# Where a kernel converts the second layer's float64 weights: beside the fourth chunk, or beside the second and third

## The chip, the cores and the metric

The kernel runs on one core of one Trainium2 chip. The metric is the device time of one execution in microseconds (us). The engines are TensorE (PE; PEld is its weight load), VectorE (DVE), ScalarE (ACT), GpSimd (POOL) and SyncE (SP), which here issues every DMA. Each engine has its own queue and works through it in order; semaphores tie them together.

## What is computed

Attention in which a query sees only the keys of its own hash bucket, and behind it two feed-forward layers:

```python
def _attn_ref(q, k, v, proj):                    # q, k, v: 2 x 8 x 768 x 64
    q_bits = (np.einsum('bhsd,dk->bhsk', q, proj) > 0)   # 6 bits; k_bits likewise
    mask = q_bucket[:, :, :, None] == k_bucket[:, :, None, :]
    scores = np.where(mask, scale * q @ k.T, -1e9)
    ...
    return np.matmul(softmax(scores), v)

x = attn_out.transpose(0, 2, 1, 3).reshape(1536, 512)
h = np.maximum(x @ w_in, 0.0)                    # layer one: 512 -> 2048 -> 512
x = h * h @ w_out
h = x @ w_in2                                    # layer two
out = (np.maximum(h, 0) + alpha * np.minimum(h, 0)) @ w_out2
```

The four weight matrices come as float64, since the reference divides them by a float64 number; q, k, v and the result are float32.

## The kernel before

**Tiling.** The 1536 tokens go in four chunks of T = 384 (NCH = 4). A layer's weights are cut into 16 steps f (KFF = 16), each with one tile of the first matrix (o = 0) and one of the second (o = 1), 128 partitions by 512 columns; a tile is named by u = (layer, f, o), so a layer has 32.

**A feed-forward chunk** is `feed_forward(l, c, background)`. For each f it splits two weight tiles into a high and a low part (`split`, L496, `split_w`, L457: ScalarE writes the high part, L462, VectorE or POOL the low one, L463), multiplies the hidden block in three products (`hidden`, L510 to L512), forms the activation in a high and a low part (L518 to L528; L528 on POOL), and multiplies the block of the step before into the accumulator (`project`, L538, L539, L542). At its end VectorE and ScalarE copy the accumulator out (L592, L594).

**Where weights come from.** `fetch(i)` (L476) brings the tiles of step i, two steps ahead of their use. In the first chunk of layer one they are converted: `load_bits` (L431) reads 512 KB of float64 as pairs of 32-bit words, `to_f32` (L437) makes float32 of them: ScalarE scales the upper words into `we` (L444), VectorE takes the sign (L446), joins the upper bits of the lower word (L447) and joins the two (L448). The result goes to DRAM (`w_d`, L494), and the later chunks of layer one read it from there (L488). `keep(u)` (L452) does the same conversion for a tile of layer two and leaves it in SBUF until the end.

**What runs beside what.** `Background(steps, marks)` holds a list of steps, and marks that say how many of them have to have run by which time; time counts in chunks, a chunk has 16 x 5 = 80 slots, and each call of `step()` in `feed_forward` moves it by one slot. The first chunk's attention runs alone. Attention for chunks two to four runs beside the layer-one chunks one to three, each ready at 0.8 of the chunk before (LEAD). Beside the fourth chunk and the first 0.3 of layer two's first chunk run the 32 `keep` steps (L649), and `second_x`, which transposes a layer-one result for layer two, at 0.3 to 0.7 of a chunk.

**Buffers.** `weight_pools` makes the pools for weights: `whole` holds four float32 tiles, `conv` the conversion's `we` and `wsg`, `wide` the tiles of 512 KB (three while attention runs, eight later). When attention is over, its pools and these are closed, and made anew with other sizes; `res` then holds the 32 kept tiles.

Of the kernel before, what the change touches and what calls it, by code (L numbers as in the profile page):

```python
# [7 lines left out]
F32 = mybir.dt.float32  # L8
# [21 lines left out]
def kernel(  # L30
# [20 lines left out]
    nc = tc.nc  # L51
    B, H, D, S = qT.shape
    NB = N_BITS
    NT, DM = out.shape
    P = 128
# [4 lines left out]
    NCH = NT // T  # L60
    KDM = DM // P
    KFF = w_in1.shape[0]
# [4 lines left out]
    def pool(name, bufs, stack=ctx, **kw):  # L67
        return stack.enter_context(tc.tile_pool(name=name, bufs=bufs, **kw))

    const = pool("const", 1)  # L70
    dram = pool("scr", 1, space=DRAM)
# [3 lines left out]
    ps_m = pool("ps_m", 2, space=PSUM)  # L75
    m1 = pool("m1", 1)
    m2 = pool("m2", 2)
    weights = ctx.enter_context(ExitStack())
    att = ctx.enter_context(ExitStack())
    state = {"attention": True, "moe": False, "s": 0, "m": 0, "h": 0}  # L80

    def weight_pools(stack, late):

        if not late:
            state["whole"] = pool("whole", 4, stack)
        state["conv"] = pool(f"conv{late}", 1 + late, stack)
        state["parts0"] = pool(f"parts0{late}", 2 + late, stack)
        state["parts1"] = pool(f"parts1{late}", 2, stack)
        state["wide"] = pool(f"wide{late}", 8 if late else 3, stack)

    weight_pools(weights, 0)
    p1 = pool("p1", 1, att)
    p2 = pool("p2", 2, att)
# [333 lines left out]
    w_d = {}  # L427
    kept = {}
    y_d = {}

    def load_bits(u):  # L431
        l, f, o = u
        t = state["wide"].tile([P, DM, 2], U32, tag="wide", name="wbits")
        nc.sync.dma_start(out=t.rearrange("p n b -> p (n b)"), in_=(WO if o else WI)[l][f].bitcast(U32))
        w_bits[u] = t

    def to_f32(u, w):  # L437


        if u not in w_bits:  # L440
            load_bits(u)
        t = w_bits.pop(u)
        e = state["conv"].tile([P, DM], F32, tag="we", name="we")
        nc.scalar.activation(e, t[:, :, 1].bitcast(F32), AF.Copy, scale=2.0 ** -112)  # L444
        s = state["conv"].tile([P, DM], U32, tag="wsg", name="wsg")
        nc.vector.tensor_scalar(s, t[:, :, 1], 0x80000000, None, ALU.bitwise_and)  # L446
        nc.vector.scalar_tensor_tensor(s, t[:, :, 0], 29, s, ALU.logical_shift_right, ALU.bitwise_or)  # L447
        nc.vector.scalar_tensor_tensor(  # L448
            w.bitcast(U32), e.bitcast(U32), 3, s, ALU.logical_shift_left, ALU.bitwise_or
        )  # L450

    def keep(u):  # L452

        kept[u] = state["res"].tile([P, DM], F32, name="w%d_%d_%d" % u)
        to_f32(u, kept[u])

    def split_w(u, engine):  # L457
        w = w_f.pop(u)
# [10 lines left out]
    def units(i):  # L469

        if i >= len(work):
            return []
        l, c, f = work[i]
        return [(l, f, o) for o in range(2)]

    def fetch(i):  # L476

        for u in units(i):
            if u in kept:
                w_f[u] = kept[u]  # L480
            elif u in w_d:
                if state["attention"]:
                    w = state["whole"].tile([P, DM], F32, tag="wf", name="wf")
                else:

                    w = state["wide"].tile([P, DM, 2], U32, tag="wide", name="wf")
                    w = w.rearrange("p n b -> p (n b)")[:, 0:DM].bitcast(F32)
                nc.sync.dma_start(out=w, in_=w_d[u])  # L488
                w_f[u] = w
            else:  # L490
                w_f[u] = state["whole"].tile([P, DM], F32, tag="wf", name="wf")
                to_f32(u, w_f[u])
                w_d[u] = dram.tile([P, DM], F32, tag="w%d_%d_%d" % u, name="w%d_%d_%d" % u)
                nc.sync.dma_start(out=w_d[u], in_=w_f[u])  # L494

    def split(i, o):  # L496
        for u in units(i)[o:o + 1]:
            split_w(u, nc.gpsimd if o or i // KFF == 1 else nc.vector)

    def hidden(l, c, f, x, step):  # L500
        xh, xl = x
        wih, wil = w_split.pop((l, f, 0))
        ps = h_tile()
        hp = ps[:, 0:T]
        for kk in range(KDM):
            if kk == KDM // 2:
                step()
            ks = slice(kk * P, (kk + 1) * P)
            first, last = kk == 0, kk == KDM - 1
            nc.tensor.matmul(hp, wih[:, ks], xh[:, kk, :], start=first, stop=False)  # L510
            nc.tensor.matmul(hp, wih[:, ks], xl[:, kk, :], start=False, stop=False)  # L511
            nc.tensor.matmul(hp, wil[:, ks], xh[:, kk, :], start=False, stop=last)  # L512
        r = m1.tile([P, T], F32, tag="r", name="r")
        g = m1.tile([P, T], F32, tag="g", name="g")
        gh = m2.tile([P, T], F32R, tag="gh", name="gh")
        gl = m2.tile([P, T], F32R, tag="gl", name="gl")
        if l == 0:
            nc.scalar.activation(r, hp, AF.Relu)  # L518
            nc.scalar.activation(gh, r, AF.Square)  # L519
            if SQUARE[c] == "a":  # L520
                nc.scalar.activation(g, r, AF.Square)
            else:
                eng[SQUARE[c]].tensor_tensor(g, r, r, ALU.mult)
        else:
            nc.vector.tensor_scalar(r, hp, 0.0, alpha_sb[:, f:f + 1], ALU.min, ALU.mult)  # L525
            nc.vector.scalar_tensor_tensor(g, hp, 0.0, r, ALU.max, ALU.add)  # L526
            nc.scalar.activation(gh, g, AF.Copy)  # L527
        nc.gpsimd.tensor_tensor(gl, g, f32(gh), ALU.subtract)  # L528
        return gh, gl
# [28 lines left out]
    def feed_forward(l, c, background):  # L558

        slots = KFF * 5  # L560
        state["slot"] = 0

        def step():
            state["slot"] += 1
            background(state["slot"] / slots)

        x = xT.pop((l, c) if l else c)
        pend = None
        acc = None
        for f in range(KFF):  # L570
            i = index[l, c, f]
            split(i + 1, 0)
            split(i, 1)
            g = hidden(l, c, f, x, step)
            fetch(i + 2)
            for u in units(i + 3):
                if u not in w_d and u[0] == 0:
                    load_bits(u)
            step()
            if pend is not None:  # L580
                if acc is None:
                    acc = ps_a.tile([P, 3, 512], F32, tag="acc", name="acc")
                project(l, *pend, acc, step)
            pend = (f, g)
        project(l, *pend, acc, step)
        y = m1.tile([P, NTB, DM], F32, tag="y", name="y")
        if l == 0:
            d = dram.tile([P, NTB, DM], F32, tag=f"y{c}", name=f"y{c}")
            y_d[c] = d
        for t in range(NTB):  # L590
            if t % 2 == 0 or l and c == NCH - 1 and t == NTB - 1:
                nc.vector.tensor_copy(y[:, t, :], acc[:, t, :])  # L592
            else:
                nc.scalar.activation(y[:, t, :], acc[:, t, :], AF.Copy)  # L594
            if l:
                s0 = c * T + t * P
                nc.sync.dma_start(out=out[s0:s0 + P, :], in_=y[:, t, :])
        if l == 0:
            nc.sync.dma_start(out=d, in_=y)
# [33 lines left out]
    steps, marks = [], [(0.0, 0)]  # L633
    for c in range(1, NCH):
        steps += attention(c, 1)
        marks.append((c - 1 + LEAD, len(steps)))
    following = Background(steps, marks)
    for c in range(NCH - 1):
        feed_forward(0, c, lambda x: following(c + x))
    following(NCH)  # L640
    att.close()
    weights.close()
    weight_pools(ctx, 1)
    state["res"] = pool("res", 1)
    state["attention"] = False


    steps = [lambda f=f, o=o: keep((1, f, o)) for f in range(KFF) for o in range(2)]
    conversion = Background(steps, [(0.0, 0), (1.3, len(steps))])  # L649
    for n in range(NCH + 1):  # L650
        steps = second_x(n) if n < NCH else []
        turned = Background(steps, [(0.3, 0), (0.7, len(steps))])
# [75 lines left out]
```

## Time and profile before

| | us |
|---|---|
| median of three runs | 870.07 |
| lowest and highest of the three | 867.12, 870.68 |
| the profiled execution, its own time | 869.21 |
| span of that execution, first to last instruction | 867.4 |
| TensorE, VectorE, ScalarE, POOL busy in it | 810.9, 552.7, 480.6, 378.6 |

Busy time of TensorE is the time covered by its matmuls, whose ends are modelled, since they overlap; it is no measure of how near to its peak it works. A group of instructions is named by its line in the kernel, its engine, and the tiles that it writes and reads (`wsg<-wbits`). Behind the bar stand its busy time, the mean of one in ns, the engine's idle time just before it, and what ended that idle time.

### The profile page before, as it was taken

The numbers are of one execution on the slowest core, as the hardware profiler recorded it, in microseconds if no ns is written. First come the engines' busy times: TensorE is split into PE (matmuls) and PEld (weight loads), VectorE is DVE, ScalarE is ACT, GpSimd is POOL, SyncE is SP. The second block draws the span as 40 slices with busy tenths as digits, with TensorE's granted clock in tenths as the row PEclk, the third lists the DMA queues.
The fourth block names the chain that finished last, engine by engine and source line by source line (L and its number), as shares of the span: only waits on it lengthen the run. The fifth ranks groups of instructions, "written<-read, shape, count | busy, mean of one in ns | idle before, by whom it ended". The sixth has DMA issues, their size and how long they took to land.

```text
span 867.4 us, 12076 instructions
## 1 busy us (share of the span) xinstructions
PE 810.9 (93%) x4192; PEld 653.4 (75%) x4192; DVE 552.7 (64%) x854; ACT 480.6 (55%) x925; POOL 378.6 (44%) x328
## 2 busy tenths in 40 slices
PE   5998998899999999999999998868999999999996
PEld 3655677676768778778777877647998998998995
DVE  6989899997666345366454599978445444444442
ACT  5668668776656556557555656654444444444331
POOL 3011233432646556433332554475555555554553
PEclk7999999999999999999999999989999999999999
DMA  7442766664332233342223777750010010000000
GB/s 232 139 133 96 254 183 210 223 203 133 112 129 71 88 110 80 89 126 85 71 82 88 274 234 259 262 215 37 1 37 37 0 38 37 1 1 37 1 0 37
DMA packets 42989, 96.40 MB, mean 111 GB/s; under 512 B 5200, under 2 KB 13744, under 8 KB 42928
## 3 DMA queue, kind: packets, MB, share of 16 engines
q1 hardware_dynamic: 42928, 95.63, 34.2%
q8 instruction: 33, 0.54, 0.3%
q14 instruction: 28, 0.23, 0.1%
HBM read 80.88 MB, written 14.73 MB: 110 GB/s over the span
## 4 chain that ended last, share of the span: by engine, by line
PE 59%; DVE 9%; issue 4%; ACT 3%; DMA 3%; POOL 2%; SPq 0%; POOLq 0%; DVEq 0%; ACTq 0%
PE acc L542 8%; PE acc L538 7%; PE acc L539 7%; PE m L329 5%; PE h L510 4%; PE h L512 4%; PE h L511 4%; PE m L313 4%; PE m L512 3%; PE m L510 3%; PE m L511 3%; PE s L292 2%; PE s L293 2%; DVE wsg L447 2%; DVE wl L463 2%
## 5 line engine op out<-in xcount | busy, mean ns | idle before, releaser
L528 POOL TENSOR_TENSOR gl<-g,gh 128x384 fp32r<-128x384 f32 x128 | 142.6, 1114 | 266.3 <-ACT gh L527 122.2
L538 PE MATMUL acc<-wh,gh 128*128 128x512 f32 x384 | 162.0, 422 | 12.6 <-ACT gh L519 10.2
L463 POOL TENSOR_TENSOR wl<-wf,wh 128x512 fp32r<-128x512 f32 x80 | 107.7, 1347 | 119.3 <-ACT wh L462 109.0
L539 PE MATMUL acc<-wl,gh 128*128 128x512 f32 x384 | 152.2, 396 | 0.0
L542 PE MATMUL acc<-wh,gl 128*128 128x512 f32 x384 | 117.2, 404 | 9.0 <-POOL gl L528 8.9
L462 ACT ACTIVATE wh<-w 128x512 fp32r<-128x512 f32 x128 | 80.4, 629 | 74.8 <-PE m L511 40.3
L462 ACT ACTIVATE wh<-wf 128x512 fp32r<-128x512 f32 x128 | 79.5, 627 | 56.0 <-PE h L511 28.9
L510 PE MATMUL h<-xh,wh 128*128 128x384 f32 x296 | 107.2, 362 | 1.1 <-ACT xh L357 0.8
L511 PE MATMUL h<-xl,wh 128*128 128x384 f32 x296 | 101.0, 341 | 0.6 <-POOL xl L358 0.6
L512 PE MATMUL h<-xh,wl 128*128 128x384 f32 x296 | 101.2, 342 | 0.0
L296 DVE TENSOR_REDUCE low<-s 128x1 f32<-128x768 f32 x84 | 80.1, 954 | 29.4 <-PE s L293 28.7
L538 PEld LDWEIGHTS acc<-wh,gh 128*128 128x128 f32 x384 | 72.6, 189 | 31.1 <-ACT gh L519 13.0
L542 PEld LDWEIGHTS acc<-wh,gl 128*128 128x128 f32 x384 | 71.9, 190 | 30.8 <-POOL gl L528 15.2
L299 ACT ACTIVATE sm<-s,low 128x768 f32<-128x768 f32 x84 | 75.3, 896 | 27.4 <-DVE low L296 27.1
L313 PE MATMUL m<-ident,sm 128*128 128x128 f32 x528 | 83.0, 274 | 5.8 <-DVE bits L215 4.0
L463 POOL TENSOR_TENSOR wl<-w,wh 128x512 fp32r<-128x512 f32 x64 | 83.9, 1310 | 8.9 <-ACT wh L462 8.6
L313 PEld LDWEIGHTS m<-ident,sm 128*128 128x128 f32 x528 | 65.5, 140 | 21.8 <-DVE bits L215 4.9
L539 PEld LDWEIGHTS acc<-wl,gh 128*128 128x128 f32 x384 | 72.9, 190 | 9.7 <-issue 1.2
L527 ACT ACTIVATE gh<-g 128x384 fp32r<-128x384 f32 x64 | 33.5, 524 | 83.6 <-DVE g L526 83.6
L525 DVE TENSOR_SCALAR r<-m,alpha_sb 128x384 f32<-128x384 f32 x43 | 26.5, 617 | 82.3 <-PE m L512 82.1
L319 DVE COPY pt<-m 128x384 f32<-128x384 f32 x112 | 61.4, 552 | 23.3 <-PE m L313 23.0
L512 PE MATMUL m<-xh,wl 128*128 128x384 f32 x216 | 72.9, 338 | 0.5 <-DVE wl L463 0.5
(105 smaller groups left out, 1568.6 us busy)
## 6 DMA issues: line engine op xcount, KB each, us to landing
wf<-w SPq DMA_DIRECT2D x96, 256.0 KB
wbits<-in_w_in_dram SPq DMA_DIRECT2D x32, 512.0 KB
wbits<-in_w_out_dram SPq DMA_DIRECT2D x32, 512.0 KB
w<-wf SPq DMA_DIRECT2D x32, 256.0 KB
qr<-in_qT_dram SPq DMA_DIRECT2D x32, 192.0 KB
kr<-in_kT_dram SPq DMA_DIRECT2D x8, 384.0 KB
qn<-in_qT_dram SPq DMA_DIRECT2D x16, 192.0 KB
vr<-in_v_dram SPq DMA_DIRECT2D x8, 384.0 KB
```

Source lines behind the costliest of these rows:

```text
L296: nc.vector.tensor_reduce(low, ps[:, 0:2, 0:HALF], AX.XY, ALU.max, negate=True)
L299: nc.scalar.activation(sm.rearrange("p (a n) -> p a n", a=2), ps[:, 0:2, 0:HALF], AF.Exp, bias=low, accum_out=self.sums[:, i:i + 1],)
L313: nc.tensor.transpose(ps[:, i * P:(i + 1) * P], pp[:, b * P:(b + 1) * P], ident)
L462: nc.scalar.activation(hi, w, AF.Copy)
L463: engine.tensor_tensor(lo, w, f32(hi), ALU.subtract)
L510: nc.tensor.matmul(hp, wih[:, ks], xh[:, kk, :], start=first, stop=False)
L511: nc.tensor.matmul(hp, wih[:, ks], xl[:, kk, :], start=False, stop=False)
L512: nc.tensor.matmul(hp, wil[:, ks], xh[:, kk, :], start=False, stop=last)
L528: nc.gpsimd.tensor_tensor(gl, g, f32(gh), ALU.subtract)
L538: nc.tensor.matmul(acc[:, t, :], gh[:, blocks[t]], woh, start=first, stop=False)
L539: nc.tensor.matmul(acc[:, t, :], gh[:, blocks[t]], wol, start=False, stop=False)
L542: nc.tensor.matmul(acc[:, t, :], gl[:, blocks[t]], woh, start=False, stop=last)
```

## The change

The conversion of the 32 tiles of layer two moves out of the fourth chunk. A second list of background steps, beside attention, loads and converts them between the times 1.0 and 2.9, that is beside the second and third layer-one chunk (`ahead`), and stores the float32 tile in DRAM. The conversion's last step now writes over its own input `we`. In the fourth chunk `keep` only reads the stored tile, from 0.25 of the chunk to 0.3 of the next. The pool `whole` now lives until the end, and the later `conv` pool has one buffer in place of two.

```diff
+    state_whole = pool("whole", 4)
...
-        if not late:
-            state["whole"] = pool("whole", 4, stack)
-        state["conv"] = pool(f"conv{late}", 1 + late, stack)
+        state["conv"] = pool(f"conv{late}", 1, stack)
...
-    def to_f32(u, w):
+    def to_f32(u, w=None):
...
+        w = e if w is None else w
         nc.vector.scalar_tensor_tensor(
             w.bitcast(U32), e.bitcast(U32), 3, s, ALU.logical_shift_left, ALU.bitwise_or
         )
+        return w
+
+    def ahead(u):
+
+        w = to_f32(u)
+        w_d[u] = dram.tile([P, DM], F32, tag="w%d_%d_%d" % u, name="w%d_%d_%d" % u)
+        nc.sync.dma_start(out=w_d[u], in_=w)
 
     def keep(u):
 
         kept[u] = state["res"].tile([P, DM], F32, name="w%d_%d_%d" % u)
-        to_f32(u, kept[u])
+        nc.sync.dma_start(out=kept[u], in_=w_d[u])
...
+    steps = []
+    for f in range(KFF):
+        for o in range(2):
+            steps += [lambda u=(1, f, o): load_bits(u), lambda u=(1, f, o): ahead(u)]
+
+    conversion = Background(steps, [(1.0, 0), (NCH - 1.1, len(steps))])
+
+    def beside(x):
+        following(x)
+        conversion(x)
+
     for c in range(NCH - 1):
-        feed_forward(0, c, lambda x: following(c + x))
+        feed_forward(0, c, lambda x: beside(c + x))
+    conversion(NCH)
     following(NCH)
...
     steps = [lambda f=f, o=o: keep((1, f, o)) for f in range(KFF) for o in range(2)]
-    conversion = Background(steps, [(0.0, 0), (1.3, len(steps))])
+    conversion = Background(steps, [(0.25, 0), (1.3, len(steps))])
```

## Rows read from the trace of the kernel before

**Rows 1.** The page: span, and each engine's busy time.

```profile
span 867.4 us, 12076 instructions
PE 810.9 (93%) x4192; PEld 653.4 (75%) x4192; DVE 552.7 (64%) x854; ACT 480.6 (55%) x925; POOL 378.6 (44%) x328
```

**Rows 2.** Busy time by stretch: from:to, length, each engine's busy time (instructions).

```profile
core 0: us, PE busy (x) PEld busy (x) DVE busy (x) ACT busy (x) POOL busy (x), PEclk, DMA share, GB/s
110.00:210.00 100.00, 92.31 (x518) 70.98 (x516) 95.65 (x153) 75.84 (x151) 34.05 (x29) 1.00 0.60 191
244.80:376.10 131.30, 129.74 (x709) 99.87 (x708) 66.66 (x102) 75.92 (x153) 70.58 (x65) 1.00 0.32 93
376.10:490.30 114.20, 113.93 (x626) 89.38 (x625) 55.63 (x95) 61.97 (x126) 40.03 (x35) 1.00 0.38 115
490.30:586.40 96.10, 77.52 (x358) 64.11 (x357) 87.59 (x111) 60.14 (x118) 51.72 (x34) 0.95 0.70 240
586.40:657.30 70.90, 68.19 (x343) 60.52 (x343) 39.14 (x64) 30.15 (x53) 36.71 (x32) 1.00 0.06 23
657.30:726.30 69.00, 68.65 (x350) 61.66 (x349) 31.42 (x53) 29.55 (x52) 36.47 (x33) 1.00 0.07 24
```

**Rows 3.** Groups of instructions in the fourth chunk, 490.3 to 586.4 us.

```profile
L448 DVE SCALAR_TENSOR_TENSOR w<-we,wsg 128x512 uint32<-128x512 uint32 x29 | 28.8, 995 | 1.9
L528 POOL TENSOR_TENSOR gl<-g,gh 128x384 fp32r<-128x384 f32 x16 | 26.5, 1654 | 39.7 <-ACT g L521 32.3 <-DMA wbits<-in_w_in_dram 4.2 <-DMA wf<-w 3.3
L447 DVE SCALAR_TENSOR_TENSOR wsg<-wbits,wsg 128x512 uint32<-128x512 uint32 x29 | 26.0, 903 | 0.6
...
L538 PE MATMUL acc<-wh,gh 128*128 128x512 f32 x48 | 20.7, 431 | 10.2 <-ACT gh L519 10.2
...
L446 DVE TENSOR_SCALAR wsg<-wbits 128x512 uint32<-128x512 uint32 x29 | 16.9, 588 | 0.1
```

**Rows 4.** Waits in the fourth chunk: us in total, times, longest.

```profile
ACT we L444 <- DMA wbits<-in_w_in_dram: 13.5, 7, 3.6
...
ACT we L444 <- DMA wbits<-in_w_out_dram: 6.4, 5, 2.5
```

**Rows 5.** Single lines, whole span: duration min/median/max in ns, first and last start.

```profile
L444 ACT ACTIVATE we<-wbits x64: 651/674/705, 23.3 to 593.7; 128x512 f32<-128x512 f32 x64
L446 DVE TENSOR_SCALAR wsg<-wbits x64: 385/423/1419, 39.8 to 598.2; 128x512 uint32<-128x512 uint32 x64
L447 DVE SCALAR_TENSOR_TENSOR wsg<-wbits,wsg x64: 647/691/1792, 40.3 to 598.6; 128x512 uint32<-128x512 uint32 x64
L448 DVE SCALAR_TENSOR_TENSOR w<-we,wsg x32: 676/692/1796, 494.4 to 600.1; 128x512 uint32<-128x512 uint32 x32
```

**Rows 6.** In order of time: start and duration in us, around two hand-overs.

```profile
488.42 0.33 PE L510 MATMUL m<-xh,wh 128*128 128x384 f32 x1
490.33 0.69 DVE L592 COPY y<-acc 128x512 f32<-128x512 f32 x1 [1.02 <-ACT y L594]
...
652.52 0.33 PE L510 MATMUL h<-xh,wh 128*128 128x384 f32 x1
657.29 0.69 DVE L592 COPY y<-acc 128x512 f32<-128x512 f32 x1 [0.66 <-ACT y L594]
```

**Rows 7.** Groups of instructions in the first chunk, 110 to 210 us.

```profile
L313 PE MATMUL m<-ident,sm 128*128 128x128 f32 x129 | 20.0, 275 | 4.6 <-DVE bits L215 4.0 <-ACT sm L299 0.3 <-DVE pt L319 0.2
L448 DVE SCALAR_TENSOR_TENSOR wf<-we,wsg 128x512 uint32<-128x512 uint32 x21 | 17.3, 826 | 2.5 <-POOL wl L463 1.8
...
L292 PE MATMUL s<-k,q 128*128 128x384 f32 x40 | 15.0, 375 | 2.6 <-ACT sm L299 2.5
```

**Rows 8.** Waits in the first chunk, 110 to 210 us.

```profile
ACT we L444 <- DVE wf L448: 7.2, 8, 2.3
```

**Rows 9.** The DMA queue's own waits in the second chunk, 244.8 to 376.1 us.

```profile
SPq L488 <- POOL wl L463: 79.6, 27, 5.8
```

**Rows 10.** POOL's groups in the first layer-two chunk, 586.4 to 657.3 us.

```profile
L528 POOL TENSOR_TENSOR gl<-g,gh 128x384 fp32r<-128x384 f32 x16 | 16.5, 1033 | 30.7 <-ACT gh L527 30.7
```

More of the change, by code (lines that the diff above doesn't have):

```diff
@@ L77 @@
     m2 = pool("m2", 2)
+    state_whole = pool("whole", 4)
     weights = ctx.enter_context(ExitStack())
     att = ctx.enter_context(ExitStack())
-    state = {"attention": True, "moe": False, "s": 0, "m": 0, "h": 0}
+    state = {"attention": True, "moe": False, "s": 0, "m": 0, "h": 0, "whole": state_whole}
     def weight_pools(stack, late):
-        if not late:
-            state["whole"] = pool("whole", 4, stack)
-        state["conv"] = pool(f"conv{late}", 1 + late, stack)
+        state["conv"] = pool(f"conv{late}", 1, stack)
         state["parts0"] = pool(f"parts0{late}", 2 + late, stack)
```

## The prediction

> **What bounds the kernel now.** I read the page's shares first: TensorE is busy for 93% of the span, VectorE for 64%, ScalarE for 55% [rows 1]. A share over the whole span hides stages, so the next view is busy time by stretch, cut where the last eviction of each feed-forward chunk begins [rows 2]. The layer-one chunks two and three last 131.3 and 114.2 us, and in them TensorE is idle for 131.3 − 129.74 = 1.6 and 0.3 us: they are as long as their matmuls. The steady layer-two chunk lasts 69.0 us with 0.35 us idle; it is the same feed-forward, with 12 transposes beside it and nothing else. The fourth layer-one chunk has the same matmuls and lasts 96.1 us: TensorE idles 18.6 us and had a mean granted clock of 0.95, so for a part of it the lower of the two levels, 1.2 instead of 2.4 GHz, which no chunk without such idling shows; VectorE is busy for 87.59 of the 96.1. So that chunk is bound by something else, and the groups of instructions in it say what: the three VectorE steps of the weight conversion take 28.8 + 26.0 + 16.9 = 71.7 us there, and TensorE's idle time sits in front of L538 (10.2 us) and is ended by ScalarE, whose queue is held up in its turn [rows 3]: its conversion step waited 13.5 + 6.4 us for the float64 bits, at most 3.6 us at once [rows 4]. The change addresses that stage.
>
> **What the fourth chunk gives back.** Removed there: all of rows 3's conversion steps. VectorE's work falls from 87.6 to 87.6 − 71.7 = 15.9 us, ScalarE's from 60.1 by some 29 steps of 0.674 us (the median of L444) to about 40 us [rows 2, 3, 5], and none of them is next to bind: TensorE's own 68 to 69 us is [rows 2]. The price of this chunk without conversion is then the steady chunk's 69.0 us, and the first layer-two chunk, which carries the last conversions and lasts 70.9 us, falls to 69.0 too: 27.1 + 1.9 = 29.0 us. One part of that may stay away. In the steady state the next chunk's first matmul starts 4.8 us ahead of the eviction that I cut at (652.52 against 657.29), at the hand-over to the fourth chunk only 1.9 us ahead (488.42 against 490.33) [rows 6]; if that stays as it is, the gain is 29.0 − 2.9 = 26.1 us. I take 27.5, midway.
>
> What is added to the fourth chunk is a read of a float32 tile per weight tile, 256 KB by its shape (128x512 float32). Between 0.25 and 1.3 of the chunk 32 are read, so 0.75/1.05 × 32 = 23 fall into it. With the 32 first-layer tiles, also of 256 KB, and 1.6 MB of y and yb that is about 16 MB in 70 us, 230 GB/s; the chunk now carries 240 GB/s at a DMA share of 0.70 [rows 2]. I cost it at nothing; if the reads were late all the same, the cover that is gone is TensorE's 0.35 us of slack, and each microsecond of lateness would be paid in full. The reads wait for nothing on SP but the space of the attention stage, which is free by then. The starting mark at 0.25 keeps them off the first reads of the chunk.
>
> **What the second and third chunk pay.** Added there are 32 conversions: a 512 KB load, one ScalarE step and three VectorE steps, and a 256 KB store. By the medians of the whole kernel one costs 0.674 us of ScalarE and 0.423 + 0.691 + 0.692 = 1.81 us of VectorE [rows 5]. Over 1.9 chunks 16.8 fall into chunk two and 15.2 into chunk three. VectorE then has 66.7 + 30.4 = 97 us of 131 and 55.6 + 27.4 = 83 us of 114, ScalarE 87 and 72 us [rows 2]. No engine passes TensorE's time. But TensorE has no slack, and VectorE works in order: a score's maximum or a hash's bits can now stand behind up to 1.81 us of conversion, so part of it shows on TensorE.
>
> The kernel has a stretch that tells the price: the first chunk between 110 and 210 us does first-layer conversions beside attention and feed-forward, the same mixture. VectorE is 95.65% busy and TensorE idles 7.69 us [rows 2]; the idle time sits in front of the transposes (4.6 us, VectorE's hash bits late) and the scores (2.6 us, softmax late) [rows 7]. With 21 conversions (the count of L448 there) that is 0.37 us each, for 32 of them 11.7 us. This is the upper end. The lower is zero; below it there is nothing to win, since chunks two and three have 1.6 + 0.3 us of idle time in all. VectorE will be at 73 to 74% there, not 96%, which speaks for less; the loads come later than in that stretch, which speaks for more (next paragraph). I take 7.5 us, a little above the middle.
>
> Two waits are new. The conversion now writes in place, so the next ScalarE step has to wait until the store of the tile before it has landed; behind that step stand the weight splits, the squares and the exponentials of ScalarE, and TensorE behind those. In the stretch 110 to 210 this step already waited for VectorE's last step 8 times, 7.2 us in all [rows 8], inside the 0.37 us; conversions there came every 4.8 us, here one comes every 7.8 and 6.8 us (1.9 chunks for 32). So I cost the longer wait at nothing, and name it as a part of the upper end. On SP a load of bits now stands right behind a store, and the store waits for VectorE: one step runs per 2.4 of a chunk's 80 slots, so the load precedes its use by 3.9 and 3.4 us. The weight reads, queries and keys of the chunk queue behind the store as well. SP has room: in chunk two its weight reads waited 79.6 us for POOL to free their buffers [rows 9], so a store that is ready earlier costs them nothing.
>
> A price from the other side: in the fourth chunk a conversion is dear because POOL and VectorE lengthen each other. POOL's L528 takes 1654 ns on average there [rows 3] and 1033 ns in the first layer-two chunk [rows 10], L447 and L448 903 and 995 ns [rows 3] where the shortest are 647 and 676 [rows 5]. TensorE lost 18.58/29 = 0.64 us per conversion in it [rows 2, 3]. The Trainium skill, in "SBUF — State Buffer", section "SBUF: two separate sides", says that these two engines share one pair of ports which is not divided but locked for a whole instruction, by a two-input VectorE step as by a POOL one. By that rule the conversions go from a stage with little POOL work to chunk two, where POOL does more, and 0.64 would be nearer than 0.37; the rows agree that the steps stretch, but none shows how far in chunk two. In rows: POOL has 70.6 us in chunk two, 51.7 us (lengthened) in the fourth [rows 2], and 32 × 0.64 = 20.5 us is the price of the second rival.
>
> **The sum**, against the profiled execution's 869.21 us (span 867.4 and 1.8 around it [rows 1]): −27.5 + 7.5 = −20.0, so 849.2. The median of the runs is 870.07, 0.86 above the profiled one, so 850 us.
>
> **The rivals.** (1) The conversions hide fully, as the 26% of VectorE that stay free would have it: 0 to 3 us paid, −26 to −29 gained, 841 to 845. Against it: TensorE's idle time is near zero, so nothing absorbs a late maximum. (2) POOL and VectorE hold each other up in chunk two as in the fourth: 20.5 us paid, 870 − 27.5 + 20.5 = 863. For it: POOL's higher load in chunk two; against it: VectorE at 74% where the fourth chunk had 91%. (3) Slower: ScalarE stands at its conversion step until the bits land, because SP can issue a load only after the store before it. The fourth chunk's waits of that kind are 19.9/12 = 1.66 us each [rows 4]; at each of 32 conversions that is 53 us of ScalarE. It decides from the point where TensorE takes over more than 27.5/53, half of it; all of it gives 870 − 27.5 + 53 = 895. Against it: ScalarE keeps 44 us free in chunk two and 42 in three, and TensorE's queue has about one feed-forward step between a hidden block and its use. (4) The change does not do what it says: were the reads to come too late for layer two, its own fetch would read the stored tile; by the marks tile pair f+2 is asked for long before, so I give it nothing.
>
> **How the numbers follow.** Forecast 0.62 (845 to 857: the ends 26.1 to 29.0 and 3 to 11.7, with a microsecond for the runs), rival 1 0.14, rival 2 0.17 (857 to 866), rival 3 0.05; 0.02 lies between 866 and 874. The range 842 to 862 leaves out the fastest of rival 1, the slower half of rival 2 and rival 3, under 0.2. A measurement of this kernel can tell about 0.5% from no change, 4.4 us: faster means below 865.7. Faster 0.62 + 0.14 + 0.15 = 0.91, same 0.05, slower 0.04.
>
> **What would show it.** Right: the fourth chunk at 69 to 72 us with TensorE idle under 3 us, no L444 in it; the first layer-two chunk at 69; chunks two and three together 5 to 10 us longer, their idle time in front of scores and transposes and ended by VectorE or by a softmax. Rival 2 shows in L528 and L463 on POOL over 1.5 us and TensorE waiting for L528's tile; rival 3 in ScalarE's waits for wbits, over 1 us at most conversions. Wrong altogether: a fourth chunk above 75 us, with ScalarE or the splits waiting for weight reads.

## The result, and the profile after

The changed kernel takes 860.06 us (median; 859.57 to 862.11) against 868.71 us of the kernel before, both of four executions: a ratio of 0.990, 95% interval 0.988 to 0.992. It is faster by 9 us, 1%, where 20 were forecast. The profiled execution takes 860.03 us, its span 858.1. Cut at the same evictions as [rows 2]:

| stretch | before, us | after, us | difference |
|---|---|---|---|
| first feed-forward chunk, from its first matmul at 90.9 | 153.9 | 151.2 | −2.7 |
| second | 131.2 | 151.6 | +20.4 |
| third | 114.3 | 116.0 | +1.7 |
| fourth | 96.0 | 69.9 | −26.1 |
| first of layer two | 70.9 | 69.4 | −1.5 |
| the rest | 205.3 | 205.4 | 0.1 |

The fourth chunk and the one behind it give back 27.6 us, the first three take 19.4. Busy time by stretch, with the columns of [rows 2], from the second chunk to layer two's first:

```profile
core 0: us, PE busy (x) PEld busy (x) DVE busy (x) ACT busy (x) POOL busy (x), PEclk, DMA share, GB/s
242.10:393.80 151.70, 137.78 (x728) 105.73 (x728) 122.15 (x168) 89.45 (x180) 78.61 (x67) 0.98 0.57 185
393.80:509.80 116.00, 114.32 (x625) 89.06 (x624) 70.38 (x120) 66.87 (x134) 40.87 (x35) 1.00 0.51 157
509.80:579.70 69.90, 68.69 (x347) 61.41 (x346) 16.46 (x24) 44.07 (x86) 37.08 (x34) 1.00 0.60 208
579.70:649.10 69.40, 69.05 (x353) 62.22 (x352) 30.29 (x54) 29.52 (x52) 36.26 (x33) 1.00 0.06 23
```

Read the second row first: TensorE idles 151.70 − 137.78 = 13.9 us where it idled 1.6, and VectorE is busy for 122.15 us. It had 66.66 before, and 97 were reckoned. The third row has 70.38 us on VectorE, where 83 were reckoned. So the conversions do not lie where the marks put them. The SP line that stores a converted tile says the same (duration in ns, first and last start):

```profile
L457 SPq DMA_DIRECT2D w<-we x32: 319/326/1380, 212.0 to 447.3; - x32
```

The first store goes out at 212 us, 30 us ahead of the end of the first chunk, the last at 447, when the third chunk has 62 us to go. By ScalarE's conversion step 4 conversions start in the first chunk, 20 in the second and 8 in the third. The order in each engine's queue is not the text's: a planner in the framework sets it, and here it queued conversions ahead of their marks.

The groups of the conversion in the second chunk, and the low part of g on POOL and TensorE's scores beside them (a count can miss a record):

```profile
L446 DVE SCALAR_TENSOR_TENSOR wsg<-wbits,wsg 128x512 uint32<-128x512 uint32 x19 | 22.4, 1179 | 0.5
L448 DVE SCALAR_TENSOR_TENSOR we<-we,wsg 128x512 uint32<-128x512 uint32 x20 | 19.5, 975 | 6.4 <-ACT we L443 6.4
L445 DVE TENSOR_SCALAR wsg<-wbits 128x512 uint32<-128x512 uint32 x19 | 14.6, 769 | 0.3
L535 POOL TENSOR_TENSOR gl<-g,gh 128x384 fp32r<-128x384 f32 x16 | 19.6, 1223 | 0.8
L291 PE MATMUL s<-k,q 128*128 128x384 f32 x54 | 20.3, 376 | 8.4 <-ACT sm L298 4.1 <-DVE k L246 2.2 <-DVE bits L214 1.8
```

and in the third chunk:

```profile
L448 DVE SCALAR_TENSOR_TENSOR we<-we,wsg 128x512 uint32<-128x512 uint32 x9 | 7.4, 825 | 7.3 <-ACT we L443 7.3
L446 DVE SCALAR_TENSOR_TENSOR wsg<-wbits,wsg 128x512 uint32<-128x512 uint32 x8 | 5.5, 685 | 0.1
L445 DVE TENSOR_SCALAR wsg<-wbits 128x512 uint32<-128x512 uint32 x8 | 4.1, 506 | 0.1
```

One conversion costs VectorE 1179 + 975 + 769 = 2.92 us in the second chunk and 2.02 in the third. POOL works 78.61 us in the one, 40.87 in the other. The largest part of TensorE's idle time, 8.4 us, sits in front of the scores (L291, which is L292 of before), ended by the softmax, the keys and the hash bits: steps of ScalarE and VectorE that stood behind others. TensorE hardly waits for POOL's tile. Four of the second chunk's waits (total, times, longest):

```profile
ACT sm L298 <- DVE low L295: 12.1, 12, 3.1
...
ACT we L443 <- DMA w<-we: 7.9, 5, 2.2
...
PE s L291 <- ACT sm L298: 4.1, 5, 1.5
...
PEld acc L549 <- POOL gl L535: 0.6, 1, 0.6
```

Not all of the 20.4 us is idle time: TensorE is busy for 137.78 us where it was for 129.74. Nineteen more matmuls fall into the chunk (728 against 709), so some work only moved over from the first. And the mean granted clock is 0.98 where it was 1.00, so for a part of the chunk it was at the lower of its two levels, 1.2 in place of 2.4 GHz. Between 262 and 272 us TensorE idles for 3.1 of the 10 us, and in the next 10 the granted clock is 0.87.

### The profile page after: what moved, and what is told of

It reads as the page before. It is cut to its first block, busy times and chain, and to the rows that moved or that the text cites. A ratio compares the mean times of both kernels' runs of the same rounds, so it can differ in the third digit from the quotient of the medians.

```text
span 858.1 us, 12213 instructions
## 1 busy us (share of the span) xinstructions
PE 807.1 (94%) x4192; PEld 653.5 (76%) x4192; DVE 548.7 (64%) x854; ACT 481.2 (56%) x925; POOL 370.6 (43%) x328
## 4 chain that ended last, share of the span: by engine, by line
PE 55%; DVE 10%; ACT 5%; DMA 4%; issue 4%; POOL 1%; SPq 0%; POOLq 0%; DVEq 0%; ACTq 0%
PE acc L549 8%; PE acc L545 7%; PE acc L546 7%; PE m L519 4%; PE m L517 4%; PE m L518 4%; PE h L517 4%; PE h L519 4%; PE h L518 4%; PE m L328 3%; DMA w<-we 3%; DVE we L448 2%; PE m L312 2%; PE s L291 2%; DVE low L295 1%
## 5 line engine op out<-in xcount | busy, mean ns | idle before, releaser
L535 POOL TENSOR_TENSOR gl<-g,gh 128x384 fp32r<-128x384 f32 x128 | 135.4, 1058 | 259.3 <-ACT gh L534 123.1
L470 POOL TENSOR_TENSOR wl<-wf,wh 128x512 fp32r<-128x512 f32 x80 | 106.3, 1330 | 131.0 <-ACT wh L469 119.0
L549 PE MATMUL acc<-wh,gl 128*128 128x512 f32 x384 | 114.7, 396 | 1.8 <-POOL gl L535 1.8
L470 POOL TENSOR_TENSOR wl<-w,wh 128x512 fp32r<-128x512 f32 x64 | 82.7, 1292 | 6.0 <-ACT wh L469 6.0
L291 PE MATMUL s<-k,q 128*128 128x384 f32 x168 | 63.0, 375 | 16.0 <-ACT sm L298 9.2
```

The lines of the kernel that those rows point to most:

```text
L291: nc.tensor.matmul(ps[:, a, 0:HALF], self.q1[:, h, qs], self.k1[:, h, ks], start=True, stop=False)
L470: engine.tensor_tensor(lo, w, f32(hi), ALU.subtract)
L549: nc.tensor.matmul(acc[:, t, :], gl[:, blocks[t]], woh, start=False, stop=last)
```

## The experiments

The measure is the end of the third chunk, since all behind it is the same in nearly every run. "Price" is that end less the 491.6 us of e5, where no conversion runs. Before has no price to pay there (490.3); the changed kernel ends the third chunk at 509.8, a price of 18.2. One kernel traced twice, as e4 and as e16, ended it at 502.1 and 499.7, so the price of one execution is good to 2 or 3 us. The times of the changed kernel, e13 and e16 are medians of four executions, the others of one; places and price are always of one traced execution. In the table, places are the conversions begun in the first, second and third chunk.

| run | total, us | third chunk ends | price | places |
|---|---|---|---|---|
| changed kernel | 860.0 | 509.8 | 18.2 | 4, 20, 8 |
| e1, result over the bits | 867.0 | 516.9 | 25.3 | 8, 24, 0 |
| e2, no VectorE steps | 855.1 | 505.0 | 13.4 | 7, 25, 0 |
| e3, one-input steps | 850.8 | 500.4 | 8.8 | 4, 20, 8 |
| e4, POOL relieved | 852.2 | 502.1 | 10.5 | 4, 20, 8 |
| e5, no conversion | 842.0 | 491.6 | 0 | none |
| e6, loads and stores only | 841.5 | 491.1 | −0.5 | none |
| e7, loads paced | 866.7 | 516.2 | 24.6 | 2, 16, 14 |
| e8, later, loads paced, POOL relieved | 858.7 | 504.2 | 12.6 | 0, 11, 20 |
| e9, no conversion, POOL relieved | 843.3 | 493.2 | 1.6 | none |
| e10, POOL's share moved to the third | 859.6 | 509.0 | 17.4 | 4, 19, 9 |
| e11, POOL relieved, short VectorE steps | 848.7 | 498.7 | 7.1 | 5, 20, 7 |
| e12, POOL relieved, result over the bits | 857.2 | 507.1 | 15.5 | 7, 25, 0 |
| e13, POOL relieved, ScalarE's step paced | 847.0 | 494.9 | 3.3 | 1, 16, 15 |
| e14, no conversion, POOL's share in the third | 841.9 | 491.6 | 0.0 | none |
| e15, ScalarE's step paced | 851.6 | 501.3 | 9.7 | 1, 16, 15 |
| e16, e4 timed | 849.5 | 499.7 | 8.1 | 4, 19, 9 |

In e8 the last conversion falls into the fourth chunk. The traced execution of e13 took 844.9 us, the fastest of its four.

**Is it the conversion at all, and is it the traffic?**

e5_no_conversion:

```diff
-            steps += [lambda u=(1, f, o): load_bits(u), lambda u=(1, f, o): ahead(u)]
+            pass
...
-        nc.sync.dma_start(out=kept[u], in_=w_d[u])
+        nc.sync.dma_start(out=kept[u], in_=w_d[(0,) + u[1:]])
```

> The second layer's conversion is left out altogether, its loads and stores too; the fourth chunk reads the first layer's stored tiles in its place (layer two computes with other weights). This is what the change could give if the conversion cost nothing beside the second and third chunk. All theories that put the loss on the conversion: the first three chunks as before (399 us from 90.9 to the third chunk's end), in all 840 to 843 us. If the loss came from the other parts of the change (the pool that lives longer, the reads): above 850 us.

Measured: 842.0 us. The first two chunks and the third:

```profile
90.90:377.30 286.40, 274.10 (x1478) 210.68 (x1476) 200.48 (x306) 186.22 (x370) 128.46 (x113) 0.99 0.46 143
377.30:491.60 114.30, 114.03 (x627) 89.41 (x626) 55.66 (x96) 61.95 (x126) 40.11 (x35) 1.00 0.38 116
```

The pool that lives longer and the reads in the fourth chunk cost nothing; the loss is the conversion's.

e6_dma_only, as e5 with loads and stores:

```diff
-        w = to_f32(u)
-        w_d[u] = dram.tile([P, DM], F32, ...)
-        nc.sync.dma_start(out=w_d[u], in_=w)
+        t = w_bits.pop(u)
+        d = dram.tile([P, DM], U32, ...)
+        nc.sync.dma_start(out=d, in_=t.rearrange("p n b -> p (n b)")[:, 0:DM])
```

> As before this one, but the 32 loads of 512 KB run beside the second and third chunk, and of each the first half is stored to a tile that nobody reads; no ScalarE or VectorE step. Theory D (DMA traffic and SP's queue): 10 us or more of the 19.4 appear, 850 us and above. Theories L and V: under 3 us, 842 to 845 us.

Measured: 841.5 us. Theory D falls: 25 MB more (32 loads of 0.52 MB and 32 stores of 0.26) on the same queue cost nothing that shows.

**Store wait or VectorE.**

e1_out_in_wide:

```diff
-        w = e if w is None else w
+        w = t.rearrange("p n b -> p (n b)")[:, 0:DM].bitcast(F32) if w is None else w
```

> The conversion writes its result into the buffer of the float64 bits instead of over we, so ScalarE's next conversion step no longer waits for a store to land; nothing else changes. The theories say of the 19.4 us that the first three chunks lost together in the changed kernel (profile against profile): theory S (ScalarE's queue stands behind the store): about half of it comes back, 850 us. Theory L (POOL and VectorE hold each other up in the second chunk), theory V (VectorE's time alone, since it works in order) and theory D (the added DMA traffic): no gain beyond 2 us, 858 to 862 us.

Measured: 867.0 us, worse by 7, which no theory had. With `we` free before the store the planner queued all 32 conversions into the first two chunks. The result now also holds one of the three buffers of the bits until it is stored, and in the second chunk ScalarE and VectorE wait for bits, 9.0 us in seven waits, where the changed kernel has none. So the run doesn't isolate the store wait, and whether the denser places or the late bits made it slower isn't shown. The same edit on e4 repeats both:

e12_light_out_in_wide: e4's edit and e1's.

> e4_pool_light with the result written into the buffer of the bits, as in e1_out_in_wide, so that ScalarE doesn't wait for a store. Theory S for the rest of the price: 846 to 849 us. Otherwise, and since the conversions then stand denser in the queues: 852 us or more.

Measured: 857.2 us against 852.2 of e4, again with 32 in the first two chunks, and with 9.6 us of waits for bits in the second.

e2_no_vector: `to_f32` returns `e` behind ScalarE's step.

> The three VectorE steps of the second layer's conversion are left out (ScalarE's scaled words are stored, so layer two computes with other weights); loads, ScalarE step, store, reads stay. Theories L and V: the first three chunks fall back to nearly the length of before, the price from 19.4 to under 4 us, the whole to 841 to 845 us. Theories S and D: the price stays above 12 us, 853 us or more.

Measured: 855.1 us and a price of 13.4, though VectorE has no conversion step: what theories S and D said, against L and V. As e6 puts D aside, it speaks for S, ScalarE's step and its wait for the store. But without VectorE's steps the conversions move ahead once more, 7 and 25, and ScalarE waits 12 times, 16.0 us in all, for a store in the second chunk, against 7.9 in the changed kernel. Since the places changed, the run can't be set against the changed kernel step by step; it says that ScalarE's step and its wait are no small matter when they stand dense.

e3_reduce:

```diff
+        if w is None:
+            m = state["conv"].tile([P, 2], F32, tag="wm", name="wm")
+            nc.vector.tensor_reduce(m[:, 0:1], t[:, :, 1].bitcast(F32), AX.X, ALU.max)
+            nc.vector.tensor_reduce(m[:, 1:2], t[:, :, 1].bitcast(F32), AX.X, ALU.max)
+            nc.vector.tensor_reduce(e[:, 0:1], e[:, 1:DM], AX.X, ALU.max)
+            return e                                 # the first layer's tiles go on to the three real steps
```

> The three VectorE steps of the second layer's conversion are replaced by three reductions over 512 elements of one input, of about the same length in all (layer two computes with other weights). VectorE is busy as long as before, but each step reads one operand. Theory L: POOL's steps in the second chunk go back to the lengths of before (about 1025 ns for the low part of g against 1223), and the price falls to half or less, 850 us or lower. Theory V: the price stays, 858 to 862 us.

Measured: 850.8 us, with the same places as the changed kernel. The three VectorE groups and POOL's L541 (the low part of g) in the second chunk:

```profile
L446 DVE TENSOR_REDUCE wm<-wbits 128x1 f32<-128x512 f32 x20 | 13.6, 681 | 14.8 <-DMA wbits<-in_w_in_dram 7.7 <-DMA wbits<-in_w_out_dram 7.1
L448 DVE TENSOR_REDUCE we<-we 128x1 f32<-128x511 f32 x20 | 13.5, 674 | 5.2 <-ACT we L443 5.1
L447 DVE TENSOR_REDUCE wm<-wbits 128x1 f32<-128x512 f32 x20 | 13.5, 674 | 0.0
...
L541 POOL TENSOR_TENSOR gl<-g,gh 128x384 fp32r<-128x384 f32 x16 | 16.2, 1014 | 0.8
```

Three steps of 0.68 us make 2.03 us, more than the 1.81 us of the real ones undisturbed [rows 5], and yet the price is halved, from 18.2 to 8.8: POOL's step is back at 1014 ns from 1223, and VectorE's don't stretch, 681 and 674 ns. Theory L holds for half of the price. The waits for bits in front of L446, 14.8 us, are new in this run and part of what it still pays. Since both engines' steps became shorter at once, the run doesn't say which of the two costs more.

**POOL's load, from its own side.**

e4_pool_light:

```diff
-SQUARE = "apva"
+SQUARE = "aava"
...
-            split_w(u, nc.gpsimd if o or i // KFF == 1 else nc.vector)
+            split_w(u, nc.gpsimd if o else nc.vector)
```

> In the second chunk the square of g goes from POOL to ScalarE, and the low parts of the first matrix's tiles go from POOL to VectorE, as in the other chunks; POOL falls from 79 to about 45 us there, VectorE gains 11 us and ScalarE 8. Theory L: the price falls by 8 us or more, 848 to 852 us. Theory V: more VectorE work makes it no better, 860 us or more.

Measured: 852.2 us; timed as e16, 849.5 us (849.06 to 849.78), a ratio of 0.976, interval 0.974 to 0.978. Theory L holds here too; theory V, which saw no gain, doesn't.

e9_no_conversion_light: e5's edit and e4's.

> e5_no_conversion with POOL relieved in the second chunk as in e4_pool_light (layer two computes with other weights). It is the control to e4: if that kernel won because POOL no longer stands in the conversion's way, the same edit is worth nothing where there is no conversion: 842 us within 1.5. If the edit is good by itself: 838 us or less.

Measured: 843.3 us, no gain. The edit is worth 8 to 10.5 us with the conversion and nothing without it.

e10_pool_swapped: as e4, with POOL's larger share in the third chunk (`SQUARE = "aapa"`, `i // KFF == 2`).

> The changed kernel with POOL's larger share (the square of g and the low parts of the first matrix's tiles) moved from the second chunk to the third. Theory L: the second chunk pays for its 20 conversions as in e4_pool_light (140 to 142 us long), and the third pays more than there for its 8: 2.9 becomes 5 to 7 us against 114.3; in all 852 to 857 us. Theory that the second chunk is dear by itself (it prepares keys): the second chunk stays above 147 us and the third at 116.

e14_no_conversion_swapped: e5's edit and e10's.

> The control to e10_pool_swapped: POOL's larger share in the third chunk and no conversion (layer two computes with other weights). If the third chunk of e10 was longer because of the conversions in it: 114 to 116 us here, 842 to 844 in all. If POOL's share alone makes it longer: 119 us or more.

Measured: 859.6 and 841.9 us. The third chunk of e10, and below it the one of e14:

```profile
385.30:509.00 123.70, 116.02 (x628) 90.94 (x627) 61.02 (x93) 67.53 (x135) 73.03 (x65) 0.99 0.48 151
```

```profile
376.70:491.60 114.90, 114.17 (x626) 89.50 (x625) 40.87 (x65) 62.13 (x126) 70.61 (x65) 1.00 0.35 115
```

With POOL at 73 us, nine conversions cost the third chunk 123.7 − 114.9 = 8.8 us, 1 us each; in the changed kernel, with POOL at 41 us, eight cost it 116.0 − 114.3 = 1.7, 0.21 each. The second chunk fell to 141.7 us, as theory L said. So the loss moved with POOL's work: the second chunk isn't dear by its keys. In all nothing was won, though: 859.6 us, where theory L said 852 to 857, since the third chunk paid more than its 5 to 7 us.

It did not move by longer two-input steps, either. These are VectorE's and POOL's steps in e10's third chunk:

```profile
L448 DVE SCALAR_TENSOR_TENSOR we<-we,wsg 128x512 uint32<-128x512 uint32 x9 | 8.0, 886 | 13.9 <-ACT we L443 13.8
L446 DVE SCALAR_TENSOR_TENSOR wsg<-wbits,wsg 128x512 uint32<-128x512 uint32 x9 | 7.6, 850 | 0.2
L445 DVE TENSOR_SCALAR wsg<-wbits 128x512 uint32<-128x512 uint32 x9 | 6.9, 771 | 0.2
...
L535 POOL TENSOR_TENSOR gl<-g,gh 128x384 fp32r<-128x384 f32 x16 | 17.2, 1074 | 1.2
```

In e4's third chunk, where POOL is busy for 42 us and the conversions cost 2.9 us in all, L448 takes 971 ns, L446 855 and POOL's L535 1088: no less. Only L445 is shorter there, 504 ns. What differs more is a wait: VectorE stands 13.8 us in front of L448 for ScalarE's step, against 4.4 in e4.

**What the other half is.**

e11_light_short_vector: e4 with e3's reductions over 8 elements.

> e4_pool_light with the three VectorE steps of each conversion replaced by reductions over 8 elements (layer two computes with other weights); ScalarE's step, the load, the store and the wait for it stay, at nearly the same places in the queues. What is left of the price in e4 (10.5 us against the kernel without conversion) is VectorE's time in order (theory V): it falls under 3 us, 842 to 845 us. Or ScalarE's step and its wait for the store (theory S): it stays above 7 us, 849 us and more.

Measured: 848.7 us, third chunk at 498.7; over its control e9 that is 5.5 us, where e4 pays 8.9 and its repeat e16 6.5. It lies between the two expectations: 1 to 3 us of what e4 pays are VectorE's time, no more than the spread of one execution; the rest remains with ScalarE's step and its wait, beside waits for bits (14.8 us in the second chunk) that this run alone of the two has.

e7_paced:

```diff
+    def load_behind(u):
+        if "read" in state:
+            with tc.issue_after(state["read"].ins):  # the latest read of a first-layer tile
+                load_bits(u)
...
-            steps += [lambda u=(1, f, o): load_bits(u), ...
+            steps += [lambda u=(1, f, o): load_behind(u), ...
```

> Each load of bits is queued on SP behind the latest read of a first-layer tile, so that the conversions stand in the engines' queues where the marks put them: 16 in the second chunk and 16 in the third, where the changed kernel has 4 in the first, 20 in the second and 8 in the third. Theory P (the price comes from the place, since the steps were queued ahead of their marks into the chunk that can bear them least): the price falls from 19.4 to 10 us or less, 850 us or lower. Theory that only the number counts: no change, 858 to 862 us.

Measured: 866.7 us, against theory P; but the waits of the second chunk tell why:

```profile
DVE wsg L453 <- DMA wbits<-in_w_in_dram: 9.6, 5, 4.1
DVE wsg L453 <- DMA wbits<-in_w_out_dram: 8.5, 5, 5.9
ACT we L451 <- DMA wbits<-in_w_in_dram: 8.4, 4, 3.2
ACT we L451 <- DMA wbits<-in_w_out_dram: 4.9, 4, 2.8
```

Held back, the loads land late, VectorE stands for 18.1 us and ScalarE for 13.3 at a conversion whose bits aren't there. In these waits the step begins 3.4 to 5.5 us behind the issue of its load, near the 3.9 and 3.4 us of lead that the prediction reckoned. That is rival 3's wait, brought about by the experiment; the changed kernel has no such waits, as its loads go ahead too, 14 to 27 us ahead of ScalarE's step.

e15_step_paced:

```diff
-        nc.scalar.activation(e, t[:, :, 1].bitcast(F32), AF.Copy, scale=2.0 ** -112)
+        scaled = lambda: nc.scalar.activation(e, t[:, :, 1].bitcast(F32), AF.Copy, scale=2.0 ** -112)
+        if w is None:
+            with tc.issue_after(state["split"].ins):
+                scaled()                             # behind the latest split
...
-        nc.scalar.activation(hi, w, AF.Copy)
+        state["split"] = nc.scalar.activation(hi, w, AF.Copy)
```

> The changed kernel with the same pacing, POOL not relieved. Theory L: with 15 in place of 24 conversions in the first two chunks, at 0.7 us each there and 0.2 to 0.4 in the third: 10.5 + 5 = 15 us of price in place of 18, 856 to 858 us. Theory P alone: 850 us or less.

Measured: 851.6 us, between the two expectations. The stores now go out where the marks say, and the first two chunks and the third read:

```profile
L462 SPq DMA_DIRECT2D w<-we x32: 319/320/1338, 247.9 to 491.5; - x32
```

```profile
90.90:382.00 291.10, 275.18 (x1480) 210.63 (x1478) 236.25 (x359) 195.94 (x387) 131.34 (x113) 0.99 0.58 191
382.00:501.30 119.30, 115.06 (x624) 89.02 (x623) 85.75 (x139) 70.56 (x141) 41.82 (x35) 1.00 0.60 193
```

The first two chunks pay 291.1 − 286.4 = 4.7 us for 17 conversions in place of 302.9 − 286.4 = 16.5 for 24; the third pays 5.0 for 15. The price is 9.7 against the 15 that place by place would give, so the conversions of the first two chunks became cheaper apiece, 0.28 us in place of 0.69. The steps in the second chunk are shorter too, though POOL is as busy there, 73.6 of 136.1 us:

```profile
L453 DVE SCALAR_TENSOR_TENSOR we<-we,wsg 128x512 uint32<-128x512 uint32 x17 | 16.0, 939 | 10.4 <-ACT we L443 10.4
L451 DVE SCALAR_TENSOR_TENSOR wsg<-wbits,wsg 128x512 uint32<-128x512 uint32 x17 | 15.3, 900 | 0.3
L450 DVE TENSOR_SCALAR wsg<-wbits 128x512 uint32<-128x512 uint32 x17 | 9.5, 557 | 0.3
L540 POOL TENSOR_TENSOR gl<-g,gh 128x384 fp32r<-128x384 f32 x16 | 16.6, 1037 | 2.1 <-issue 1.1
```

One conversion takes VectorE 2.40 us here against 2.92 in the changed kernel, and POOL's step 1037 ns against 1223. So POOL's busy time alone doesn't set how far the steps lengthen.

e13_step_paced_light: e4's edit and e15's.

> e4_pool_light with ScalarE's conversion step queued behind the latest split of a first-layer tile, so that the conversions stand 15 in the second chunk and 16 or 17 in the third, while the loads stay as early as the three buffers allow (in e7_paced the loads were held back, and VectorE stood waiting for bits). If the rest of the price comes from how dense the conversions stand (theory P): 846 to 850 us, and no waits for wbits. If only their number counts: 851 to 854 us, as e4.

Measured: 847.0 us (844.93 to 850.53), a ratio of 0.975, interval 0.972 to 0.978: in theory P's range, and without waits for bits. The price of the traced execution is 3.3 us, 1.7 over its control, but that was the fastest of four; by the median it is about 2 us more. Of the kernels that compute the whole result it is the fastest by median, 13 us under the changed kernel; from e16 it isn't set apart, as the intervals overlap.

```profile
90.90:375.60 284.70, 271.50 (x1474) 209.16 (x1473) 235.14 (x373) 200.63 (x402) 97.44 (x81) 1.00 0.60 195
375.60:494.90 119.30, 115.08 (x625) 89.05 (x624) 85.99 (x140) 70.51 (x141) 41.89 (x35) 1.00 0.59 193
```

e8_later_pool_light: e7's pacing and e4's edit, marks `[(1.5, 0), (2.99, ...)]`.

> Paced as the run before, with the marks at 1.5 and 2.99 (9 conversions in the second chunk, 21 in the third, 2 at the start of the fourth), and POOL relieved in the second chunk as in e4_pool_light. If place and POOL's load both count, both gains add: 845 to 849 us. If 21 conversions are too many for the third chunk: 852 us or more, with the loss in that chunk.

Measured: 858.7 us. The third chunk and the fourth:

```profile
381.80:504.20 122.40, 114.32 (x622) 89.40 (x622) 100.93 (x158) 72.90 (x146) 45.02 (x36) 1.00 0.69 224
504.20:578.50 74.30, 70.20 (x341) 62.42 (x342) 17.68 (x25) 44.53 (x87) 36.98 (x33) 0.98 0.64 221
```

Twenty conversions cost the third chunk 8.1 us, and the fourth, into which the last one reaches, is 4.4 us longer than in the changed kernel. The held-back loads of e7 are part of this (waits for bits of 6.8 us in the third chunk), so it says only that later is not better without limit.

e16_pool_light_timed is e4 again:

> e4_pool_light again, timed: 851 to 854 us, a ratio of 0.978 to 0.983 to the kernel before; faster than the changed kernel's 860.

Measured: 849.5 us, below what was expected; the single execution of e4 had taken nearly 3 us more.

## Why the prediction was right and wrong

**The gain in the fourth chunk was right.** 27.5 us were forecast for it and the chunk behind, 26.1 + 1.5 = 27.6 came. The fourth chunk's VectorE work was reckoned at 15.9 us and is 16.46, ScalarE's at 40 and is 44.07. The reads cost nothing, as reckoned: 208 GB/s beside 0.60 of DMA share, and TensorE idles 1.2 us. The hand-over of [rows 6] did not improve: the fourth chunk's first matmul starts at 507.85 and the eviction at 509.76, 1.9 us apart as before. By the prediction's own condition the gain should then have been 26.1 us. Only 1.4 of the 2.9 us stayed away, so that the midpoint came out is in part luck.

**The price was wrong: 7.5 us forecast, 18 to 19 measured.** The 860 us lie within the stated range of 842 to 862, but in the part of it that was rival 2's. The step that failed is the sentence "16.8 fall into chunk two and 15.2 into chunk three". It read the marks of the text as the places in the queues. 24 conversions were queued into the first two chunks, and everything behind that sentence, VectorE at 74% and the argument against rival 2 with it, was reckoned for a kernel that wasn't there. VectorE came to 122.15 of 151.70 us, 81%, and 20 of the 32 conversions met the chunk in which POOL has most to do. e15 comes near the kernel that the sentence described (17 and 15): it takes 851.6 us and pays 9.7, within the 3 to 11.7 of the forecast. The trace of before held a hint that wasn't followed up: SP issued the first read of `yb`, marked for 0.3 of the fourth chunk, at 474.7 us, while TensorE was still in the third.

**The second step that failed is the price of one, where POOL is busy.** 0.23 us each was taken, between 0 and 0.37. Where POOL is light it was right: 0.21 in the third chunk of the changed kernel, 0.33 at twice the density in e15. In the first two chunks it is 16.5/24 = 0.69, near rival 2's 0.64. That rival gave 863 and had a chance of 0.17; it came nearest in time. Its own signs did not come: POOL's steps stayed under 1.5 us (L535 at 1223 ns, L470, which is L463 of before, at 1352), and TensorE waited 0.6 us for L535's tile; the loss reached it through the softmax, the keys and the hash bits. That POOL's share of the work carries about half of the loss is shown: less work on POOL (e4 with its control e9) takes half of it away, and POOL's work moved to another chunk (e10 with its control e14) takes a part of it along. That it does so by lengthened steps is less sure: for it speaks e3, where reductions in their place halve the price; against it e10, in whose third chunk the two-input steps were no longer than in e4's, and the loss came all the same. The Trainium skill, in "SBUF — State Buffer", section "SBUF: two separate sides", says that a VectorE step with two SBUF inputs and a POOL step that reads SBUF lock each other out for a whole instruction, and that a VectorE step in a mode that takes both ports and a POOL step do so too. The trace agrees in part: 1179 ns for L446, which has two inputs, beside a POOL that is busy for 52% of the time, 685 beside one at 35%, and the reductions, which have one, stay at 674 to 681. But L445, which has one input as well, went from 506 to 769 ns; in which mode it ran no run here shows. The prediction had this page and the stretch of the fourth chunk before it, and gave it too little weight.

**The two new waits.** The wait of ScalarE for the store was put at nothing. It shows, 7.9 us in five waits in the second chunk, and 7.4 in four in the third, where the conversions cost little. The two runs that take it away (e1, e12) are slower, but they changed the places and brought waits for bits. What it costs at equal places was not isolated; e2, which pays 13.4 us without a VectorE step, and e11 say that ScalarE's step and this wait are a good part of the rest. Rival 3 didn't come, and that was luck: the loads went out 14 to 27 us ahead of their use, ahead of their marks like the conversions, and e7, where they stood near the marks, has the waits. The DMA traffic was rightly put at nothing (e6).

**What stays open.** Pacing and relief of POOL each take about half of the price, and together leave some 3 to 5 us of it (e13). How the loss divides among VectorE's lengthened steps, ScalarE's step and its wait isn't settled. Nor is why e15's conversions in the second chunk are cheaper apiece, their steps shorter beside a POOL as busy: there are fewer of them, and each now stands behind a weight split in ScalarE's queue, not anywhere ahead of a softmax; no run here changes the one without the other.

## What to carry to other kernels

Work that is moved under another engine's cover has its price in the stretch where it is queued; so check in the built queues, not in the text, where it will stand, and pin the step that holds others up (here ScalarE's), not the load that feeds it. Before VectorE work is moved to a stretch, look at POOL's work there too: here moving its share away was worth 8 to 10.5 us, though VectorE had time left in either case. A background that seems free by busy shares can be priced by the stretch of the same trace that comes nearest in all its engines, POOL too.

## What the runs showed of the hardware

Two-input VectorE steps over 128x512 words took 685 and 825 ns beside a POOL that was busy for 35% of the time, and 1179 and 975 ns beside one that was busy for 52%; a one-input `tensor_scalar` went from 506 to 769 ns with them, and POOL's 128x384 step took 1223 ns there, against 1014 beside reductions of one input. The busy share does not fix these lengths: beside POOL at 54% in e15 the two steps took 900 and 939 ns, at 59% in e10's third chunk 850 and 886. Nine conversions there made the chunk 8.8 us longer, where eight had cost 1.7. And 25 MB of loads and stores more, beside 143 and 116 GB/s that moved in the same stretches without them, cost the kernel nothing that a single execution can tell (841.5 us against 842.0).
